# Sums of squares as four rows of 112, and 1 / root spread to all partitions by a store and a load in GpSimd's queue

## The chip, the cores and the metric

The kernel runs on one core of one Trainium2 chip. The metric is the device time of one execution in microseconds. The core's engines are TensorE (PE, with its weight loads shown apart as PEld), VectorE (DVE), ScalarE (ACT) and GpSimd (POOL). Each works through its own list of instructions in the order in which the kernel was written; SyncE (SP) issues most of the transfers. A wait is a semaphore that an instruction needs before it starts.

## What is computed

Three stages in a row, on 4 batches of 448 tokens (1792 tokens) with 768 features:

```python
attn = 1 / (1 + np.exp(-(scale * q @ k.T - np.log(448))))   # 4 batches, 12 heads of 64
x = attn @ v                                                # heads side by side: 1792 x 768
rms = np.sqrt(np.mean(x * x, axis=-1, keepdims=True) + 1e-06)
xn = x / rms * rms_g
g, val = xn @ w_gate, xn @ w_val                            # 768 -> 1536, twice
x = (g * sigmoid(g) * val) @ w_out                          # 1536 -> 768
# then each token goes to the one of 8 experts with the largest logit (768 -> 1024 -> 768)
```

The change is about the line of `rms`: the sum of squares over the 768 features of a token, 1 / root of the mean, and the multiplication of x by it.

## The kernel before

Everything is kept with features on partitions and tokens along the free dimension. x of a batch is six tiles of 128 features x 448 tokens; a feature's sum over partitions can therefore not be made by VectorE, and 1 / root of a token has to stand on all 128 partitions before x can be multiplied by it.

**Attention** runs as one loop of 84 steps, 21 for each batch. A step issues four fp32 matmuls of scores (line 927) into one of two double banks, four fp32 matmuls weights x values (line 944) of the step before last, and one sigmoid on ScalarE (line 933). Both kinds of matmul use 64 x 64 pieces of the array. A group of heads takes four or three steps in turn; its sums are in two banks of a pair, `one0` and `one1` for even groups, `one2` and `one3` for odd ones. When a group ends, ScalarE copies the first bank out (line 971), VectorE adds the second to it (line 972), ScalarE squares the tile (978 or 981) and VectorE adds the square to `ss`, the batch's running sum (line 982). After that a tile of x holds 128 features x 448 tokens, and `ss` 128 partial sums for each token.

**normalise(b)** is a generator that starts at the sixth step of the next batch and goes one `yield` further in every step. For the last batch it goes on in the gated loop, one `yield` at every even slot. It sums `ss` over the partitions with four matmuls that have `ss` as weights and a column of ones as moving data (line 1013), so that the sums of 112 tokens at a time stand on 112 partitions, four columns in all, in bank `one3`. VectorE makes 1 / root of the 112 x 4 numbers in 13 small instructions (lines 1017 to 1030). ScalarE widens each to a row of 128 (`yb`, line 1033), four matmuls against the identity turn this so that each token's number stands on all partitions (line 1038, `one3` again), ScalarE copies it to `rs` (line 1040), and VectorE multiplies the six tiles of x in six steps (line 1043). For batches 2 and 3 SyncE then stores x (line 1048), because it is needed only in the second half of the network.

**Between these** VectorE has other work. A generator `conv` turns the fp64 words of the weights into fp32, three instructions for each piece (lines 217, 221 and 225), one of them in each step that has room: the sets `busy` and `scaling` in the attention loop say which steps have none, and the condition in the gated loop at which slots. SyncE stores each converted piece and loads the next. The calls in `x_at` (x_sum, x_hi, x_lo, lines 320 to 336) make sums and differences of x's tiles and split them into a high and a low part.

**The gated loop** takes batches 0 and 1 through w_gate and w_val: 12 column blocks, each of 7 slots (a Strassen form with seven products), each slot of 9 matmuls of 128 x 128 by 448 (lines 311 to 313). `window(p, n, k)` is what ScalarE and VectorE do beside slot k of block n: they take banks out, form the gate, and prepare the next products' weights (line 282 for the high part, line 287 for the low one, line 304 for sums). Line 450 is the last gate operation of a block, at slot 6; the low part that the second product after it waits for is written a few instructions later. After the gated loop come the projection w_out (`output`), the second half, and the experts.

GpSimd has 11 instructions in the whole run: constants at the start, then nothing until the routing that follows the w_out projection.

## Time and profile before

| | us |
|---|---|
| time, median of 3 runs (890.42 to 890.8) | 890.51 |
| profiled execution, its own time | 890.12 |
| its span | 888.3 |
| PE busy | 877.8 (99%) |
| DVE busy | 645.8 (73%) |
| ACT busy | 396.3 (45%) |
| POOL busy | 4.6 (1%) |

The profiled execution takes 1.8 us more than its span, which lies around the first and last instruction. The granted clock of TensorE is full in all 40 slices of the page. Of the chain that ended last 96% is PE. "Waits" in the views below are times in which an engine had nothing to do until another released it; the chain of waits is followed back from the last instruction, so what stands in it set the end.

### The profile page before, as it was taken

To read this page: it belongs to the slowest core of one execution; us is meant where nothing else is said; L and a number is where in the kernel's file an instruction comes from. 1 tells how busy PE (TensorE), PEld (TensorE's weight loads), DVE (VectorE), ACT (ScalarE), POOL (GpSimd) and SP (SyncE) were. 2 spreads that over 40 slices of the span, in tenths; PEclk is the share of its full clock that TensorE was granted. 3 is DMA by queue.
4 is the path that set the end of the run, shared out by engine and by line. 5 is a ranking of instruction groups with operands and counts; after the bars stand their busy time and mean duration, and the time that the engine had idled before them with its cause. 6 is when DMAs were issued, how large, how long until landed. Compare 5 with 4: busy or idle time off the path is not lost.

```text
span 888.3 us, 14287 instructions
## 1 busy us (share of the span) xinstructions
PE 877.8 (99%) x5376; PEld 737.1 (83%) x5376; DVE 645.8 (73%) x1154; ACT 396.3 (45%) x632; POOL 4.6 (1%) x11
## 2 busy tenths in 40 slices
PE   8999999999999999999999999999999999999997
PEld 3544447999999899999999999998899888889996
DVE  3678889898998985977988788976766644334454
ACT  6877876444445511453444545563322322322220
POOL 0000000000000000000000000000000000000000
PEclk9999999999999999999999999999999999999999
DMA  8988865265544399871212123759779679679232
GB/s 314 397 283 312 300 256 171 81 248 178 178 165 148 135 306 330 271 215 49 72 53 72 54 72 125 257 174 295 204 212 328 221 269 293 195 258 300 76 71 57
DMA packets 121228, 177.59 MB, mean 200 GB/s; under 512 B 62570, under 2 KB 82922, under 8 KB 121153
## 3 DMA queue, kind: packets, MB, share of 16 engines
q1 hardware_dynamic: 111696, 174.03, 59.2%
q10 hardware_dynamic: 9312, 2.07, 1.3%
q8 instruction: 43, 0.70, 0.3%
q0 software_dynamic: 144, 0.53, 0.2%
q14 instruction: 33, 0.26, 0.1%
HBM read 131.11 MB, written 45.35 MB: 199 GB/s over the span
## 4 chain that ended last, share of the span: by engine, by line
PE 96%; DVE 2%; DMA 0%; issue 0%; ACT 0%; SPq 0%; DVEq 0%
PE four L311 14%; PE four L313 14%; PE four L312 14%; PE one L311 12%; PE one L313 12%; PE one L312 12%; PE two L927 7%; PE one L944 7%; PE one L759 1%; DVE m L461 1%; PE four L1291 1%; PE four L1267 1%; PE one L1038 0%; PE one L1013 0%; DMA rqk<-in_qkp 0%; PE one L1291 0%
## 5 line engine op out<-in xcount | busy, mean ns | idle before, releaser
L313 PE MATMUL one<-m,wc 128*128 128x448 f32 x282 | 103.5, 367 | 0.1
L311 PE MATMUL one<-m,wc 128*128 128x448 f32 x282 | 102.6, 364 | 0.0
L312 PE MATMUL one<-m,wc 128*128 128x448 f32 x282 | 102.3, 363 | 0.0
L933 ACT ACTIVATE a<-two,logs 128x896 f32<-128x896 f32 x84 | 84.6, 1008 | 26.7 <-PE two L927 24.1
L927 PE MATMUL two<-rqk 64*64 64x448 f32 x672 | 88.0, 548 | 3.7 <-DMA rqk<-in_qkp 3.7
L944 PE MATMUL one<-a,rv 64*64 64x448 f32 x672 | 86.4, 537 | 0.0
L313 PE MATMUL four<-m,wc 128*128 128x448 f32 x213 | 78.0, 366 | 0.0
L311 PE MATMUL four<-m,wc 128*128 128x448 f32 x213 | 77.7, 365 | 0.0
L312 PE MATMUL four<-m,wc 128*128 128x448 f32 x213 | 77.6, 364 | 0.0
L312 PE MATMUL four<-m,wr 128*128 128x448 f32 x180 | 65.7, 365 | 0.4 <-DVE m L461 0.4
L311 PE MATMUL four<-m,wr 128*128 128x448 f32 x180 | 65.7, 365 | 0.0
L313 PE MATMUL four<-m,wr 128*128 128x448 f32 x180 | 65.5, 364 | 0.0
L287 DVE TENSOR_TENSOR wc<-raw,wc 128x384 fp32r<-128x384 f32 x115 | 61.6, 550 | 3.3 <-ACT wc L282 3.3
L927 PEld LDWEIGHTS two<-rqk 64*64 64x64 f32 x672 | 29.9, 135 | 39.3 <-issue 24.1
L944 PEld LDWEIGHTS one<-a,rv 64*64 64x64 f32 x672 | 30.5, 133 | 33.9 <-issue 32.3
L282 ACT CAST wc<-raw 128x384 fp32r<-128x384 f32 x115 | 55.1, 515 | 7.2 <-DMA raw<-w32d 5.4
L312 PEld LDWEIGHTS one<-m,wc 128*128 128x128 f32 x282 | 52.9, 187 | 4.7
L313 PEld LDWEIGHTS one<-m,wc 128*128 128x128 f32 x282 | 52.9, 188 | 4.1 <-DVE wc L287 0.4
L311 PEld LDWEIGHTS one<-m,wc 128*128 128x128 f32 x282 | 53.0, 188 | 3.8
L1112 ACT CAST w2h<-w2r 128x1024 fp32r<-128x1024 f32 x24 | 25.2, 1048 | 57.3 <-PE one L312 32.3
L311 PE MATMUL four<-xc,wr 128*128 128x448 f32 x126 | 46.8, 372 | 0.0
L312 PE MATMUL four<-xc,wr 128*128 128x448 f32 x126 | 46.2, 367 | 0.0
(279 smaller groups left out, 1923.2 us busy)
## 6 DMA issues: line engine op xcount, KB each, us to landing
raw<-w32d SPq DMA_DIRECT2D x67, 384.0 KB, 3.4
w32d<-wn SPq DMA_DIRECT2D x36, 384.0 KB, 3.1
w1r<-in_w SPq DMA_DIRECT2D x24, 512.0 KB, 5.9
w2r<-in_w SPq DMA_DIRECT2D x32, 384.0 KB, 6.1
x2s<-x SPq DMA_DIRECT2D x48, 224.0 KB, 4.0
rqk<-in_qkp SPq DMA_DIRECT2D x23, 448.0 KB, 6.5
w<-in_wg SPq DMA_DIRECT2D x12, 768.0 KB, 6.8
w<-in_wv SPq DMA_DIRECT2D x12, 768.0 KB, 7.1
```

Source lines behind the costliest of these rows:

```text
L282: nc.scalar.copy(out=h, in_=source(p, n, j).rearrange("p (c k) -> p c k", k=128))
L287: nc.vector.tensor_tensor(out=l, in0=w, in1=f32(h), op=ALU.subtract)
L311: nc.tensor.matmul(p, wh, xh, start=first, stop=False, **kw)
L312: nc.tensor.matmul(p, wh, xl, start=False, stop=False, **kw)
L313: nc.tensor.matmul(p, wl, xh, start=False, stop=last, **kw)
L461: nc.vector.tensor_tensor(out=t, in0=held["h", g, x][0], in1=f32(held["hs", g, x, 0][0]), op=ALU.subtract)
L759: nc.tensor.matmul(logit_bank[b][: 2 * E, :S], gate_2[:, oc, :], x2_t[b, oc][k], start=(oc == (b == B - 1) and k == 1), stop=(oc == KD - 1 ...
L927: nc.tensor.matmul(two[t % 2][o, x, :S], r[head, k : k + D], r[head, :S], start=True, stop=True)
L933: nc.scalar.activation(out=a, in_=two[t % 2][:, :, :S], func=AF.Sigmoid, bias=logs, scale=1.0 / math.sqrt(D))
L944: nc.tensor.matmul(one[2 * y + k][halves[x], :S], v4[halves[i], c, x, :], a[halves[i]], start=(c == first), stop=(c == end))
L1112: nc.scalar.copy(out=hv, in_=r)
L1267: nc.tensor.matmul(ph[TS * j : TS * j + TS], xt[:, c, :], ph2["w1f"][:, c, n * j : n * j + n], start=(c == 0), stop=(c == KD - 1),)
```

## The change

The four matmuls that sum `ss` change sides. The weights are now four columns of a new constant `part` (the c-th of four has ones in column c and zeros elsewhere), and `ss` is the moving data: 4 x 112 results accumulate in one place of `one3`, row c for tokens 112 c to 112 c + 111. The same 13 instructions of VectorE work on 4 x 112 numbers in place of 112 x 4. GpSimd's queue then stores them as 448 numbers in DRAM (`rsd`) and loads them with a broadcast into `rs`, all 128 partitions. The widening, the four turning matmuls and the two ScalarE copies are gone. x is multiplied from the seventh `yield` after that on, four steps later than before. `scaling` moves by four steps with it, one call of `x_sum` by one, and `busy` follows.

```diff
+    add("part", np.tile(np.eye(NC).reshape(1, -1), (128, 1)))
...
+    rsd = [dram.tile([1, S], F32, name=f"rsd{b}") for b in range(B)]
...
-        pm = mi[:CT, :NC]
+        pm = mi[:NC, :CT]
         for c in range(NC):
-            nc.tensor.matmul(pm[:, c : c + 1], ss[:, c * CT : (c + 1) * CT], ones[:, 0:1], start=True, stop=True)
-        va = rp.tile([CT, NC], F32, tag="va", name="va")
-        ya = rp.tile([CT, NC], F32, tag="ya", name="ya")
-        ta = rp.tile([CT, NC], F32, tag="ta", name="ta")
+            nc.tensor.matmul(
+                pm, const("part")[:, c * NC : (c + 1) * NC], ss[:, c * CT : (c + 1) * CT], start=(c == 0), stop=(c == NC - 1)
+            )
+        t = keep.tile([NC, 3, CT], F32, tag="xr", name="ya")
+        va, ya, ta = (t[:, i, :] for i in range(3))
...
         yield
-        yb = keep.tile([CT, NC, 128], F32, tag="xr", name="yb")
-        nc.scalar.copy(out=yb, in_=ya.unsqueeze(2).to_broadcast([CT, NC, 128]))
-        yield
-        yield
-        pr = mi[:, :S]
-        for c in range(NC):
-            nc.tensor.matmul(pr[:, c * CT : (c + 1) * CT], yb[:, c, :], ident[:CT, :CT], start=True, stop=True)
+        nc.gpsimd.dma_start(out=rsd[b].rearrange("o (c p) -> (o c) p", p=CT), in_=ya)
         rs = rp.tile([128, S], F32, tag="rs", name="rs")
-        nc.scalar.copy(out=rs, in_=pr)
-        yield
+        nc.gpsimd.dma_start(out=rs, in_=rsd[b].to_broadcast([128, S]))
+        for _ in range(7):
+            yield
         for c in range(KD):
...
-        60: [(x_sum, 0, P5)], 62: [(x_sum, 0, P7)], 64: [(x_hi, 0, P5, True)], 65: [(x_lo, 0, P5)],
+        61: [(x_sum, 0, P5)], 62: [(x_sum, 0, P7)], 64: [(x_hi, 0, P5, True)], 65: [(x_lo, 0, P5)],
...
-    busy = {8, 14, 18, 23, 28, 40, 43, *range(60, 73, 2), 67, 71, 81}
+    busy = {8, 14, 18, 23, 28, 40, 43, 61, *range(62, 73, 2), 67, 71, 81}
...
-        scaling = n >= QS and n % QS in (10, 12, 14)
+        scaling = n >= QS and n % QS in (14, 16, 18)
```

Step 81 stands both in `busy` and in the new `scaling`, so one more step of the attention loop has a conversion, and every later conversion comes one place earlier. Line numbers of the changed kernel are 2 higher up to the middle of `normalise` and 2 lower after it.

On TensorE, in the step of batch 1 where the turning matmuls of batch 0 stood, this is the order before (`two` and `one` are banks, `a` the weights of attention, `rv` the values):

```order
L927 MATMUL two_147<-rqk 64x448 x4
L944 MATMUL one_143<-a,rv 64x448
L944 MATMUL one_144<-a,rv 64x448 x2
L944 MATMUL one_143<-a,rv 64x448
L1038 MATMUL one_146<-cst,yb 128x112 x4
L927 MATMUL two_148<-rqk 64x448 x4
```

and now:

```order
L929 MATMUL two_151<-rqk 64x448 x4
L946 MATMUL one_147<-a,rv 64x448
L946 MATMUL one_148<-a,rv 64x448 x2
L946 MATMUL one_147<-a,rv 64x448
L929 MATMUL two_152<-rqk 64x448 x4
```

The four matmuls between the two halves of the loop are gone; the four of the sums stay at their place, with other shapes.

On VectorE, from the last of the 1 / root instructions of batch 0 to the first multiplication of x, before (`wn` is a converted weight, `m` a tile of x):

```order
L1030 SCALAR_TENSOR_TENSOR ya<-ta,ya 112x4
L217 TENSOR_SCALAR wn<-w_454 128x768
L221 SCALAR_TENSOR_TENSOR wn<-w_454,wn 128x768
L972 TENSOR_TENSOR m<-one_145,m 128x448
L225 SCALAR_TENSOR_TENSOR wn<-w_454,wn 128x768
L1043 SCALAR_TENSOR_TENSOR m<-m,ng_sb,rs 128x448
```

and now:

```order
L1033 SCALAR_TENSOR_TENSOR ya<-ta,ya 4x112
L219 TENSOR_SCALAR wn<-w_458 128x768
L223 SCALAR_TENSOR_TENSOR wn<-w_458,wn 128x768
L974 TENSOR_TENSOR m<-one_149,m 128x448
L227 SCALAR_TENSOR_TENSOR wn<-w_458,wn 128x768
L219 TENSOR_SCALAR wn<-w_502 128x768
L984 TENSOR_TENSOR ss<-ss,sq 128x448
L223 SCALAR_TENSOR_TENSOR wn<-w_502,wn 128x768
L227 SCALAR_TENSOR_TENSOR wn<-w_502,wn 128x768
L974 TENSOR_TENSOR m<-one_148,m 128x448
L219 TENSOR_SCALAR wn<-w_581 128x768
L1041 SCALAR_TENSOR_TENSOR m<-m,ng_sb,rs 128x448
```

Ten instructions stand where four stood; the first multiplication now comes behind the next group's addition (line 972, now 974) and a third conversion.

On VectorE in the gated loop, from line 450 of block 2 (now 452) on, before, with two multiplications of x of batch 3 in the block:

```order
L450 SCALAR_TENSOR_TENSOR m<-m,one_143 128x448
L287 TENSOR_TENSOR wc<-sw,wc 128x384
L1043 SCALAR_TENSOR_TENSOR m<-m,ng_sb,rs 128x448
L221 SCALAR_TENSOR_TENSOR wn<-w_1401,wn 128x768
L388 TENSOR_TENSOR c_1801<-four_1490,c_1801 128x448
L287 TENSOR_TENSOR wc<-raw,wc 128x384
L1043 SCALAR_TENSOR_TENSOR m<-m,ng_sb,rs 128x448
L225 SCALAR_TENSOR_TENSOR wn<-w_1401,wn 128x768
L400 TENSOR_TENSOR m<-c_1801,m 128x448
L401 SCALAR_TENSOR_TENSOR m<-m,c_1836 128x448
```

and now, with the first two of the four that stand in the same block:

```order
L452 SCALAR_TENSOR_TENSOR m<-m,one_147 128x448
L289 TENSOR_TENSOR wc<-sw,wc 128x384
L1041 SCALAR_TENSOR_TENSOR m<-m,ng_sb,rs 128x448
L227 SCALAR_TENSOR_TENSOR wn<-w_1352,wn 128x768
L390 TENSOR_TENSOR c_1779<-four_1475,c_1779 128x448
L289 TENSOR_TENSOR wc<-raw,wc 128x384
L1041 SCALAR_TENSOR_TENSOR m<-m,ng_sb,rs 128x448
L219 TENSOR_SCALAR wn<-w_1416 128x768
L402 TENSOR_TENSOR m<-c_1779,m 128x448
L403 SCALAR_TENSOR_TENSOR m<-m,c_1809 128x448
```

Before, four of batch 3's six multiplications stood between line 450 of blocks 1 and 2 and two between blocks 2 and 3; now none stands before line 452 of block 2, four stand between blocks 2 and 3, and two between blocks 3 and 4.

## Rows read from the trace of the kernel before

**Rows 1.** Waits of TensorE, whole span: us in total, times, longest us.

```profile
PE two L927 <- DMA rqk<-in_qkp: 3.7, 1, 3.7
PE four L312 <- DVE m L461: 0.4, 1, 0.4
```

**Rows 2.** Chain that ended last, batch 0's normalise: start us, us, what.

```profile
45.55 0.88 PE one L1013 x8
46.43 0.91 PE two L927 x8
47.34 0.75 PE one L944 x8
...
52.60 1.07 PE one L1038 x8
54.59 0.75 PE one L944 x8
```

**Rows 3.** TensorE's timeline, batch 3's normalise, gated loop: start us, us, instruction.

```profile
150.90 0.85 PE L1013 MATMUL one<-ones,ss 128*112 128x1 f32 x8
...
151.91 0.36 PE L312 MATMUL one<-m,wc 128*128 128x448 f32 x1
152.11 0.36 PE L313 MATMUL one<-m,wc 128*128 128x448 f32 x1
...
164.44 1.04 PE L1038 MATMUL one<-cst,yb 112*128 112x112 f32 x8
...
165.54 0.36 PE L312 MATMUL one<-m,wc 128*128 128x448 f32 x1
```

**Rows 4.** Weight loads by line: ns least/median/most, first and last start, shape.

```profile
L759 PEld LDWEIGHTS one<-x,gate x48: 93/94/96, 315.4 to 629.6; 128*16 128x16 f32 x48
...
L1013 PEld LDWEIGHTS one<-ones,ss x32: 173/178/179, 45.5 to 151.5; 128*112 128x112 f32 x32
```

**Rows 5.** VectorE by line: ns least/median/most, first and last start, shape.

```profile
L1017 DVE TENSOR_SCALAR va<-one x4: 152/162/163, 46.5 to 151.9; 112x4 f32<-112x4 f32 x4
...
L1043 DVE SCALAR_TENSOR_TENSOR m<-m,ng_sb,rs x24: 674/678/686, 54.3 to 183.6; 128x448 f32<-128x448 f32 x24
```

**Rows 6.** VectorE's timeline, attention, batch 1: start us, us, instruction, [idle before].

```profile
49.98 0.17 DVE L1030 SCALAR_TENSOR_TENSOR ya<-ta,ya 112x4 f32<-112x4 f32 x1
...
59.19 0.62 DVE L972 TENSOR_TENSOR m<-one,m 128x448 f32<-128x448 f32 x1 [0.68 <-ACT m L971]
...
62.24 0.62 DVE L982 TENSOR_TENSOR ss<-ss,sq 128x448 f32<-128x448 f32 x1 [0.37 <-ACT sq L981]
...
64.24 0.62 DVE L972 TENSOR_TENSOR m<-one,m 128x448 f32<-128x448 f32 x1
```

**Rows 7.** TensorE's timeline in the same place: the bank's next use.

```profile
67.94 0.93 PE L944 MATMUL one<-a,rv 64*64 64x448 f32 x8
```

**Rows 8.** GpSimd's DMA issues: tiles, queue, count, us to landing.

```profile
xg<-x2d,s_g POOLq DMA_INDIRECT x1, 7.5
out<-rows,s_s1st POOLq DMA_INDIRECT x1, 3.0
```

**Rows 9.** Windows: us, busy us (instructions) by engine, clock, DMA share, GB/s.

```profile
83.00:93.00 10.00, 10.00 (x108) 4.43 (x104) 7.59 (x16) 8.47 (x12) 0.00 (x0) 1.00 0.97 341
...
684.00:694.00 10.00, 10.00 (x51) 9.19 (x50) 8.84 (x24) 1.26 (x2) 1.12 (x1) 1.00 0.99 342
```

**Rows 10.** VectorE's timeline, gated loop, blocks 2 and 3.

```profile
180.09 0.62 DVE L450 SCALAR_TENSOR_TENSOR m<-m,one 128x448 f32<-128x448 f32 x1
...
186.22 1.02 DVE L287 TENSOR_TENSOR wc<-raw,wc 128x384 fp32r<-128x384 f32 x2
...
192.96 0.62 DVE L450 SCALAR_TENSOR_TENSOR m<-m,one 128x448 f32<-128x448 f32 x1
```

**Rows 11.** TensorE's timeline there: the matmul that reads that low part.

```profile
187.58 0.37 PE L313 MATMUL four<-m,wc 128*128 128x448 f32 x1
```

**Rows 12.** GpSimd's timeline, the first transfer of rows 8: start us, us, instruction.

```profile
686.18 1.12 POOL L1235 DMA_INDIRECT xg<-x2d,s_g  x1 [56.06 <-DMA w2r<-in_w]
```

## The prediction, blind

> **What bounds the kernel now.** I read the waits of TensorE first, over the whole span. There are three, and the two long ones are 3.7 us at the start for the first load and 0.4 us for VectorE at the end of the first gated loop [rows 1]; 96% of the chain that ended last is TensorE. The kernel is one unbroken stream of matmuls: whatever leaves the stream shortens the run by its own length, provided that the other engines, which have little room in places, still deliver in time. The chain then shows what normalise costs the stream [rows 2], the timeline of TensorE the same for the last batch, which falls into the gated loop [rows 3], and the timelines of VectorE how much room there is.
>
> **What the stream loses.** In attention a half step is 0.75 us. From the start of the four sums (45.55) to the next L944 (47.34) it takes 1.79 us where 0.75 would do, so the sums cost 1.04 us; the turning matmuls cost 54.59 - 52.60 - 0.75 = 1.24 us [rows 2]. Both figures include what the L927 behind them is longer than 0.75. The chain shows the same for the two other batches whose normalise is in attention. In the gated loop the pace is 0.20 us a matmul. There the sums start at 150.90 and the second matmul behind them at 151.91, which is 1.01 - 0.20 = 0.81 us for the sums; in the same way 165.54 - 164.44 - 0.20 = 0.90 us for the turning [rows 3]. Removing the turning matmuls gives 3 x 1.24 + 0.90 = 4.6 us.
>
> **What the new sums cost.** They remain eight instructions on TensorE, with 4 weight columns and 112 moving ones in place of 112 and 1. No row shows four columns. A load of 16 columns took 94 ns and one of 112 took 178 [rows 4], so the loads get short; the moving side becomes that of the turning matmuls, which cost 0.90 with a longer load than either. So the new sums lie between half of the old (loads alone, 0.4) and the turning (0.9), in attention between 0.5 and 1.24. I take the old cost, which is nearer to the upper row because the moving side is the same: no gain or loss here, at most 3 x 0.2 + 0.1 = 0.7 us worse or 3 x 0.5 + 0.4 = 1.9 us better.
>
> **ScalarE** loses two copies a batch. It never held TensorE up, so this is worth nothing by itself.
>
> **VectorE, the 13 small instructions.** Four numbers a partition took 0.16 us, 448 took 0.68 [rows 5]; on a straight line 112 take 0.29, so 13 instructions cost 13 x 0.13 = 1.7 us more for each batch, at most (none, if the length of the dependence hides it). VectorE waited for the sums before its L1017 in attention, so the first of them is still on time there, and 1.7 us fit into the idle time of each batch's steps. In the gated loop the room before L450 of block 1 takes them.
>
> **The store and the load.** They stand alone in GpSimd's queue, the load behind the store's landing; nothing else is queued behind them until the routing. What waits is VectorE's first L1041, and behind it on VectorE the addition that empties a bank of attention. Batch 0 as example. The last root instruction ended at 50.15 [rows 6]; with the longer instructions 51.8. The first multiplication now stands behind the addition that came at 59.19; TensorE is 1.24 earlier by then, so that addition ends at 58.5 and, behind one conversion of about half a microsecond, the multiplication is due at 59.0. That gives 7.2 us free. Behind it comes L982, which waited for ScalarE until 62.24 and now comes at 61.0: a multiplication of 0.6 us may start as late as 60.4 without delaying anything. Then the addition at 64.24, whose bank TensorE writes next at 67.94 [rows 7], has (with both 1.24 earlier) about 3.2 us before TensorE waits. So the way through DRAM may take 60.4 + 3.2 - 51.8 = **11.8 us**. The other two batches give 11 to 12 in the same manner, and the last one, in the gated loop, over 20.
>
> The only transfers that GpSimd issues before took 3.0 and 7.5 us to land [rows 8]. The long one ran while the DMA engines were 99% busy; where batch 1's pair would fall they are at 97% [rows 9]. The store is 1.8 KB, the load 224 KB and plain, with longer rows than the gathered one. I take 3.0 + 5.5 = 8.5 us, between 3.0 + 3.0 = 6.0 and 7.5 + 7.5 = 15.0. At 8.5 VectorE waits about a microsecond where it would have waited anyway, and TensorE doesn't.
>
> The page "DMA: Bandwidth & Descriptors" of the Trainium skill, section "Anatomy of one DMA — SWDGE (gpsimd) path", gives 2.0 us plus the bytes over 436 KB per us; by that the pair is an estimated 4.5 us and never late. The trace doesn't agree: 386 KB would take 2.9 us by it and took 7.5 [rows 8]. The sum would be the same by the page.
>
> **The multiplications, four steps later.** In attention each lands in steps with as many conversions moved out. At the end, batch 2's six share steps 77 to 82 with the first gated weights, but two conversions have been moved ahead; what TensorE needs first from VectorE there has about 2.5 us of room. In the gated loop it is tight. Between L450 of blocks 2 and 3 VectorE was busy without a break: 12.87 us [rows 10]. TensorE needs 12.73 for the 63 matmuls of a block (165.54 - 151.91 - 0.90 for the turning [rows 3]). Two multiplications stood there, now four: 2 x 0.68 = 1.36 us more [rows 5], so L450 of block 3 comes about 1.5 us late. The low part behind it was written 0.81 us before it was read: L287 at 186.22 took 0.55 of its 1.02, read at 187.58 [rows 10, 11]. Two long conversions stood ahead of it there; in block 4 one of the two is a short one, so that there is somewhat more. TensorE waits 1.5 - 0.81 = 0.7 us at most; I take **0.3 us**, with 0 as the other end.
>
> **The conversion that moved ahead** puts a short instruction (L217) where a long one (L221) stood at the end of that loop, in front of VectorE's only long-lasting backlog; the wait of 0.4 us [rows 1] goes, or stays.
>
> **Sum:** 4.6 + 0.4 - 0.3 = 4.7 us less. The profiled execution would go from 890.12 to 885.4, the median of 890.51 to **885.8**. The bounds of the parts give 4.6 - 0.7 - 0.7 = 3.2 to 4.6 + 1.9 + 0.4 = 6.9 less: 883.6 to 887.3, of which I believe the lower end least, since nothing but load time speaks for it.
>
> **Rivals.**
> *VectorE becomes the bound around the gated loop's first five blocks.* For it: VectorE has no idle time in blocks 2 and 3 [rows 10], the 1.7 us of longer root instructions fall just ahead, and the late L450 delays ScalarE too. If the backlog lasts through blocks 3 and 4 at 1 to 1.5 us each, TensorE waits 2 to 3 us: 888. Against it: blocks 1 and 2 become emptier by four multiplications.
> *GpSimd and VectorE stop each other.* If VectorE stood still for each GpSimd instruction (1.12 us [rows 12]), two a batch, it would lose 2.2 us a batch. Attention covers that; the last batch's would fall on blocks 0 and 1, where about 1.8 us of room is left for the root instructions' 1.7: 1.5 to 2.2 us, 887.6. That such a lock exists is what the page "SBUF — State Buffer" says, section "Who interferes with whom": GpSimd and a VectorE instruction in a two-port mode share a port pair, and the later one waits until the other is through. No row here shows the two at once.
> *The way through DRAM is late.* The point is 11.8 us; at 15.0 the addition behind the multiplication is 3.2 us late in three batches, 9.6 us in all, and the run takes 885.8 + 9.6 = **895.4**, slower than before. It decides from 11.8 + 4.7 / 3 = 13.4 us on. For it: three of the four pairs run beside weight loads that keep the DMA engines nearly full, and a GpSimd transfer did take 7.5 us under such a load [rows 8, 9]. Against it: the store is tiny, and the two rows added give 10.5.
> *The stream doesn't get shorter,* because new sums cost as much as old sums and turning together, for instance when four columns make the array run badly: 890.
>
> **How the numbers follow.** A measurement of this kernel can tell about 0.2% (1.8 us) from no change. Forecast 0.66; VectorE the bound 0.13; GpSimd against VectorE 0.06; late way 0.12, of which half reaches the slower side and the rest ends between; no shorter stream 0.03. The forecast's cases and most of the next two lie below 888.7: faster 0.83. Within 0.2%: what remains of these, part of the late way, and the last: 0.10. Slower: 0.07. The range leaves out the late way, the last rival and the low end of the sums: 884.4 to 888.6.
>
> **What would show it.** In the changed profile, TensorE's chain at batches 0 to 2 should show one piece of eight with 0.8 to 1.0 us in each batch and none of L1038; attention should end 3.5 to 4 us earlier. L1041's first wait for the load should be under 1.5 us, and no PE wait should name L974 or a bank. In the gated loop a PE wait of under 0.7 us for L289 may stand near block 4, and the wait at the end of that loop should be gone. The prediction is wrong if GpSimd's pair takes over 12 us, if the new sums cost over 1.2 us, or if PE waits for VectorE sum up to over 1.5 us.

## The result: 899.3 us, and the profile after

The changed kernel takes 899.28 us (median of 6 runs, 896.15 to 899.99), the kernel before in the same comparison 890.46 (890.07 to 890.80): a ratio of 1.0088 [1.0077, 1.0098], slower by 8.8 us where 4.7 us of gain were forecast. The time lies outside the range, on the side of the rival "the way through DRAM is late" (895.4). The profiled execution took 899.5 us, its span grew from 888.3 to 897.7.

In the waits of TensorE over the whole span (us in total, times, longest) five kinds are new, the wait for rqk (attention's loads) has grown by 0.5, and the 0.4 us at the end of the first gated loop [rows 1] is gone:

```profile
PE two L929 <- DMA rqk<-in_qkp: 4.2, 2, 3.9
PE two L929 <- ACT a L935: 2.1, 4, 0.7
PE one L313 <- ACT four L372: 2.0, 1, 2.0
PE one L313 <- ACT c L399: 1.6, 1, 1.6
PE one L946 <- DVE m L974: 0.9, 1, 0.9
PE one L1015 <- DVE ss L984: 0.4, 2, 0.3
```

(Lines have moved a little: L929, L935, L946, L974, L983 and L984 are L927, L933, L944, L972, L981 and L982 of before; L372 and L399, L370 and L397 of before, are ScalarE's copies of banks in the gated stage; L1015 are the sums, L1033 the last kind of root instruction, L1035 the store, L1037 the load, L1041 the multiplications.)

What was forecast for TensorE's own work came true. In the chain the sums of batch 0 are one piece of eight (start us, us, what), as long as the old ones, 0.88 [rows 2], and nothing stands where the turning was:

```profile
45.60 0.87 PE one L1015 x8
```

Ten of the 13 root instructions on 112 elements cost VectorE 0.26 us each in place of 0.16 [rows 5], the other three 0.20 (two kinds of the ten: line, ns least/median/most, first and last start):

```profile
L1020 DVE TENSOR_SCALAR ya<-one x4: 255/258/262, 46.5 to 159.8; 4x112 f32<-4x112 f32 x4
L1031 DVE TENSOR_TENSOR ya<-ya x12: 253/263/265, 48.7 to 164.4; 4x112 f32<-4x112 f32 x12
```

The way through DRAM did not. GpSimd's timeline (start us, us, instruction, idle before and for what) has a pair for each batch, and the windows under it, each from a store's issue to its load's, show how full the DMA engines were meanwhile (after the granted clock: DMA share, GB/s):

```profile
51.64 0.69 POOL L1035 DMA_DIRECT2D rsd<-ya  x1 [51.18 <-DVE ya L1033]
57.30 0.59 POOL L1037 DMA_DIRECT2D rs<-rsd  x1 [4.97 <-DMA rsd<-ya]
86.58 0.53 POOL L1035 DMA_DIRECT2D rsd<-ya  x1 [28.69 <-DVE ya L1033]
94.24 0.56 POOL L1037 DMA_DIRECT2D rs<-rsd  x1 [7.12 <-DMA rsd<-ya]
...
165.52 0.53 POOL L1035 DMA_DIRECT2D rsd<-ya  x1 [36.92 <-DVE ya L1033]
167.66 0.56 POOL L1037 DMA_DIRECT2D rs<-rsd  x1 [1.61 <-DMA rsd<-ya]
```

```profile
51.64:57.30 5.66, 5.66 (x64) 2.29 (x60) 5.23 (x8) 4.56 (x6) 0.69 (x1) 1.00 0.92 335
86.58:94.24 7.66, 7.66 (x88) 3.12 (x84) 6.16 (x10) 6.24 (x8) 0.53 (x2) 1.00 1.00 368
122.20:128.04 5.84, 5.84 (x68) 2.32 (x64) 5.80 (x7) 4.74 (x7) 1.05 (x1) 1.00 0.97 379
165.52:167.66 2.14, 0.81 (x4) 0.77 (x5) 1.93 (x5) 1.82 (x4) 0.53 (x2) 1.00 0.01 1
```

The store of 1.8 KB alone kept the load waiting 5.0, 7.1 and 4.8 us in attention, where the engines were 92 to 100% busy, and 1.6 us in the gated loop, where they stood idle. VectorE doesn't part the two cases: it was busy for 80 to 99% of these windows in attention and for 90% of the quiet one. The load took 3.5 to 6.8 us. From the end of the root to the first multiplication it was 12.8, 14.6 and 10.8 us in the three batches of attention; 8.5 had been taken and 11.8 allowed. VectorE's timeline shows the first multiplication of batches 0, 1 and 2 waiting:

```profile
64.13 0.68 DVE L1041 SCALAR_TENSOR_TENSOR m<-m,ng_sb,rs 128x448 f32<-128x448 f32 x1 [5.06 <-DMA rs<-rsd]
...
100.92 0.68 DVE L1041 SCALAR_TENSOR_TENSOR m<-m,ng_sb,rs 128x448 f32<-128x448 f32 x1 [5.40 <-DMA rs<-rsd]
...
132.66 0.69 DVE L1041 SCALAR_TENSOR_TENSOR m<-m,ng_sb,rs 128x448 f32<-128x448 f32 x1 [1.77 <-DMA rs<-rsd]
```

How this comes to TensorE shows in ScalarE's timeline. ScalarE's square of a head stands in its list ahead of the next sigmoids and needs VectorE's addition L974, which stood behind the waiting multiplication; so the sigmoids are late:

```profile
67.38 0.58 ACT L983 ACTIVATE sq<-m 128x448 f32<-128x448 f32 x1 [1.67 <-DVE m L974]
67.87 1.89 ACT L935 ACTIVATE a<-two,logs 128x896 f32<-128x896 f32 x2
```

TensorE, in its own timeline, waits for the first of these sigmoids:

```profile
68.91 0.98 PE L929 MATMUL two<-rqk 64*64 64x448 f32 x8 [0.54 <-ACT a L935]
```

SyncE carries it on in a second way. Its list holds the store of converted weights (L232), which waits for VectorE's conversions, and behind it the next loads for attention (rqk). After 59.9 us it stood until 69.43; in the kernel before the same store went out at 64.36 us (before, then now):

```profile
64.36 0.33 SPq L230 DMA_DIRECT2D w32d<-wn  x1
```

```profile
59.03 0.86 SPq L210 DMA_DIRECT2D w<-in_wv  x1
69.43 0.33 SPq L232 DMA_DIRECT2D w32d<-wn  x1
69.87 0.37 SPq L898 DMA_DIRECT2D rv<-in_v  x1
70.69 0.32 SPq L891 DMA_DIRECT2D rqk<-in_qkp  x1
```

### The profile page after: what moved, and what is told of

The parts are those of the page before. It is cut to its first block, busy times and chain, and to the rows that moved or that the text cites. A ratio compares the mean times of both kernels' runs of the same rounds, so it can differ in the third digit from the quotient of the medians.

```text
span 897.7 us, 14232 instructions
## 1 busy us (share of the span) xinstructions
PE 879.8 (98%) x5344; PEld 727.9 (81%) x5344; DVE 649.2 (72%) x1154; ACT 391.9 (44%) x624; POOL 9.6 (1%) x19
## 4 chain that ended last, share of the span: by engine, by line
PE 85%; DVE 8%; DMA 5%; issue 1%; ACT 0%; SPq 0%; POOLq 0%; DVEq 0%
PE four L313 14%; PE four L314 14%; PE four L315 14%; PE one L313 12%; PE one L314 12%; PE one L315 12%; PE two L929 3%; PE one L946 2%; DMA rs<-rsd 2%; DMA rsd<-ya 2%; PE one L761 1%; DVE m L1041 1%; DVE m L326 1%; DVE wn L227 1%; DVE m L974 1%
## 5 line engine op out<-in xcount | busy, mean ns | idle before, releaser
L935 ACT ACTIVATE a<-two,logs 128x896 f32<-128x896 f32 x84 | 84.2, 1007 | 26.7 <-PE two L929 25.2
L929 PE MATMUL two<-rqk 64*64 64x448 f32 x672 | 84.3, 554 | 6.3 <-DMA rqk<-in_qkp 4.2
L946 PE MATMUL one<-a,rv 64*64 64x448 f32 x672 | 82.2, 538 | 0.9 <-DVE m L974 0.9
L289 DVE TENSOR_TENSOR wc<-raw,wc 128x384 fp32r<-128x384 f32 x115 | 61.7, 550 | 5.1 <-ACT wc L284 5.1
L929 PEld LDWEIGHTS two<-rqk 64*64 64x64 f32 x672 | 26.4, 135 | 46.7 <-issue 26.7
L946 PEld LDWEIGHTS one<-a,rv 64*64 64x64 f32 x672 | 26.8, 134 | 39.1 <-issue 35.0
```

Source lines behind the costliest of these rows:

```text
L289: nc.vector.tensor_tensor(out=l, in0=w, in1=f32(h), op=ALU.subtract)
L929: nc.tensor.matmul(two[t % 2][o, x, :S], r[head, k : k + D], r[head, :S], start=True, stop=True)
L935: nc.scalar.activation(out=a, in_=two[t % 2][:, :, :S], func=AF.Sigmoid, bias=logs, scale=1.0 / math.sqrt(D))
L946: nc.tensor.matmul(one[2 * y + k][halves[x], :S], v4[halves[i], c, x, :], a[halves[i]], start=(c == first), stop=(c == end))
```

## The experiments

All are compared by one ladder: how far the same instruction of TensorE lies behind (+) or ahead of (-) its time in the profile of the kernel before, at three places. "Gated" is the first matmul of the gated stage (138.74 us before), "four" the first into the second set of banks from converted weights (147.26; behind the stage's first stall), "output" the first of the output stage (294.97). Where two or three profiles of a kernel exist, each stands. Three kernels that leave TensorE's attention as it was (before_pair, moved, before_pad) lie 0.2 to 0.4 us behind at "gated", so the ladder can't tell less than that. The rows of "gated", before and in the changed kernel's first profile:

```profile
138.74 0.47 PE L311 MATMUL one<-m 128*128 128x448 f32 x1
```

```profile
141.92 0.47 PE L313 MATMUL one<-m 128*128 128x448 f32 x1
```

| run | gated | four | output | median us | ratio to before |
|---|---|---|---|---|---|
| changed kernel | +3.2 / +0.9 / +1.1 | +5.4 / +4.6 / +4.7 | +9.6 / +5.8 / +7.8 | 899.28 | 1.0088 [1.0077, 1.0098] |
| no_dram, no_dram_2 | -3.7 / -3.3 | -1.8 / +0.2 | +0.8 / +0.7 | - | - |
| no_wait, no_wait_2 | -0.8 / -1.9 | +1.1 / +0.1 | +3.1 / +4.6 | - | - |
| before_pair | +0.4 | +0.4 | +0.4 | 890.46 | 0.9998 [0.9988, 1.0007] |
| moved | +0.4 | +3.9 | +3.9 | 894.03 | 1.0038 [1.0024, 1.0052] |
| later | +0.8 | +0.8 | +1.6 | 892.64 | 1.0025 [1.0014, 1.0036] |
| later_pool | -0.3 | -0.3 | +5.0 | 894.98 | 1.0036 [1.0019, 1.0054] |
| after_b2 | -0.6 | -0.5 | +6.7 | 897.82 | 1.0077 [1.0054, 1.0100] |
| after_b2_pool | +1.4 | +1.6 | +8.8 | 898.56 | 1.0070 [1.0049, 1.0090] |
| rows_spread | -0.1 | 0.0 | +1.0 | 893.39 | 1.0029 [1.0015, 1.0044] |
| fast_spread | +4.4 | +4.4 | +7.2 | 904.17 | 1.0146 [1.0122, 1.0171] |
| before_pad | +0.2 | +0.2 | +0.5 | 890.64 | 1.0000 [0.9989, 1.0011] |

### The wait for the roots, and the transfers without it

```diff
 no_dram
-        nc.gpsimd.dma_start(out=rsd[b].rearrange("o (c p) -> (o c) p", p=CT), in_=ya)
-        nc.gpsimd.dma_start(out=rs, in_=rsd[b].to_broadcast([128, S]))
+        nc.gpsimd.memset(rs, 0.5)
 no_wait
-                out=xt[c], in0=xt[c], scalar=ng_sb[:, c : c + 1], in1=rs, op0=ALU.mult, op1=ALU.mult
+                out=xt[c], in0=xt[c], scalar=ng_sb[:, c : c + 1], in1=ones[:, 0:1].to_broadcast([128, S]), op0=ALU.mult, op1=ALU.mult
```

> The changed kernel without the way through DRAM: GpSimd sets rs to a constant instead of the store and the load, so the roots reach nothing and x is scaled by g and a constant. All else, the new sums, the root on 112 elements and the scaling four steps later, is kept. Theory 1 (the multiplication waits for a way through DRAM that takes 11 to 15 us instead of the 8.5 of the prediction, and VectorE's wait comes back to TensorE by way of ScalarE's squares): no wait at L1041, the time falls to about 886 (885 to 888). Theory 2 (the new shape or the later steps cost the time themselves: 13 root instructions of 0.3 us in place of 0.2, scaling in among the sums for the next stage): it stays at 894 or more. Theory 3 (the GpSimd transfers get in the way of others, nobody's wait): also about 886, so the next run has to part it from theory 1.

> The changed kernel with its store and load as they are, but the multiplication takes a column of ones in place of rs: the transfers run, nobody waits for the load, and the roots reach nothing. Theory 1: within 1 us of the run without the transfers, about 886. Theory 3 (the transfers hold VectorE's port or take the DMA engines from the weights): it stays near the changed kernel, 894 to 899.

> The run without the transfers once more (the roots are replaced by a constant). No wait in the attention, which ends 3.5 to 3.9 us ahead of the kernel before, and a wait of 1.9 us at the start of the gated stage. The total again says nothing.

> The run without a wait once more (transfers as in the changed kernel, the multiplication takes ones in place of the roots). If the transfers themselves cost the attention: TensorE waits for rqk in it again and the attention ends 0 to 1.5 us ahead of the kernel before. If the first profile was chance: 3 to 4 us ahead, as without the transfers. The total says nothing, since without the roots the tokens go to other experts.

Their totals (979.7 and 982.2 us) can't be used: without the roots the routing comes out differently, and the 90 us that are added lie after 700 us (before that, no_dram is 1.0 us and no_wait 4.0 us behind). Up to there they can be read by the ladder. Without the transfers attention has not one wait of TensorE and ends 3.7 and 3.3 us ahead: the gain that was forecast for it is there. With the transfers running and nobody waiting it ends 0.8 and 1.9 us ahead, and TensorE waits for rqk, as the second profile's waits show beside those at the start of the gated stage:

```profile
PE two L929 <- DMA rqk<-in_qkp: 4.6, 2, 3.7
PE one L313 <- ACT four L372: 1.9, 1, 1.9
PE one L313 <- ACT c L399: 1.6, 1, 1.6
...
```

So the transfers by themselves cost some 2.1 us of attention (the means of two profiles each; 1.4 to 3.0), and the wait for them 3.1 us more (mean of the changed kernel's three, +1.7, against -1.4). The expected "within 1 us of the run without the transfers" failed: theory 1 alone was not enough. It failed for no_dram too, which lies 0.8 us behind at "output" where about 4.5 ahead was expected. What both runs share is a wait of 1.9 us at the start of the gated stage and one of up to 1.6 behind it, with no wait for roots anywhere, so those belong to something else.

A wait cost more than its idle time. In the changed kernel's first profile TensorE's waits in attention, without the first load's, add up to 3.9 us, but at "gated" it lies 6.9 us behind no_dram. Matmul by matmul against no_dram it falls back by 1.15 us at the wait of 0.54 us (68.9 us) and by 0.95 us at the one of 0.72 us (139.5 us). Why is not shown.

> The kernel before with the two GpSimd transfers added and nobody waiting for them: right after ScalarE's copy of the root 4 rows of 112 of that copy go to DRAM and from there to all partitions of a tile that is dead by then. Computes what the kernel before does. If the transfers crowd the loads of the attention (theory: in the run without a wait TensorE stood at rqk and attention ended 2.9 us later than without the transfers), TensorE waits for rqk once or twice, attention ends 1.5 to 3 us later and the time is 892 to 893.5. If they cost nothing by themselves and only the wait for them does: 890.5.

```diff
         nc.scalar.copy(out=yb, in_=ya.unsqueeze(2).to_broadcast([CT, NC, 128]))
+        nc.gpsimd.dma_start(out=rsd[b].rearrange("o (c p) -> (o c) p", p=CT), in_=yb[:NC, 0, :CT])
+        rx = keep.tile([128, S], F32, tag=("k0", "k1", "k3", "xs")[b], name="rx")
+        nc.gpsimd.dma_start(out=rx, in_=rsd[b].to_broadcast([128, S]))
```

In the kernel before the same two transfers cost nothing: 890.46 us, and in attention no wait but the first load's. The two results fit together if the loads of attention have about as much to spare as its steps are long: in the kernel before they come in time beside the transfers, and in a stream that is 1.24 us a batch faster they don't. That is how I read it; what the rows show is the wait for rqk in the one case and none in the other. It also speaks against the rival "GpSimd and VectorE stop each other": eight such transfers changed no time.

### The four steps

```diff
 moved: the kernel before, old sums and turning
         nc.scalar.copy(out=rs, in_=pr)
         yield
+        for _ in range(4):
+            yield
...
-        scaling = n >= QS and n % QS in (10, 12, 14)
+        scaling = n >= QS and n % QS in (14, 16, 18)
```

> The kernel before with nothing changed but the steps: its scaling four steps later, as in the changed kernel, with the old sums, root and turning matmuls. Theory 1: the roots are there 4 steps ahead, the multiplication waits for nothing, 890 to 891.5, no change. Theory 2 (the later steps are the cost): 894 or more.

This run has none of the new sums, transfers or waits for roots (the steps without a conversion and one x_sum move with the multiplications), and it loses 3.5 us (1.0038 [1.0024, 1.0052]): neither theory's number, and a cause of its own. Up to the gated stage the ladder says +0.4, no more than before_pair has; behind the stage's first stall +3.9, and it stays there. ScalarE's timeline of the kernel before (one line), the same of this run (two), and TensorE's timeline of this run (one):

```profile
140.64 0.58 ACT L981 ACTIVATE sq<-m 128x448 f32<-128x448 f32 x1 [1.99 <-DVE m L972]
```

```profile
142.96 0.58 ACT L981 ACTIVATE sq<-m 128x448 f32<-128x448 f32 x1 [3.78 <-DVE m L972]
143.44 0.53 ACT L370 COPY four<-one 128x448 f32<-128x448 f32 x1
```

```profile
144.02 0.74 PE L311 MATMUL one<-m 128*128 128x448 f32 x1 [1.87 <-ACT four L370]
```

The last heads' additions L972 now stand behind two multiplications of batch 2 and a conversion in VectorE's list; ScalarE's square waits 3.78 us for one, and the copy L370 that frees a bank for TensorE stands behind the square. The other 1.6 us are the clock. In the windows (granted clock third from the right) TensorE stood from 142.15 to 144.02 and went on at 0.50, the lower of its two levels (1.2 GHz), for 3 us:

```profile
142.00:144.00 2.00, 0.15 (x4) 0.00 (x0) 2.00 (x4) 1.04 (x3) 0.00 (x0) 1.00 0.93 339
144.00:147.00 3.00, 2.98 (x8) 2.68 (x9) 2.39 (x5) 2.46 (x4) 0.00 (x0) 0.50 0.83 250
```

The same wait of 1.9 or 2.0 us stands in the changed kernel, no_dram and no_wait. The clock fell behind it in this run, in no_dram_2 and in two of the changed kernel's three profiles, not in the others; what decides is not shown.

### More room for the way, and batch 2 alone

```diff
 later: the changed kernel
-        for _ in range(7):
+        for _ in range((11, 11, 10, 7)[b]):
             yield
 after_b2: the changed kernel
+        for _ in range((7, 7, 10, 7)[b]):
 later_pool, after_b2_pool: also
-                nc.sync.dma_start(
+                (nc.gpsimd if b == 2 else nc.sync).dma_start(
```

(In all four the steps without a conversion move as well; in later and later_pool also the copies and differences that read x for the gated stage.)

> The changed kernel with the multiplications 4 steps later still in batches 0 and 1 and 3 later in batch 2 (a step is about 1.6 us), the work that reads x for the gated stage moved behind them by as much. Computes what the changed kernel does. Theory 1: VectorE's wait at L1041 goes from 5.1, 5.4 and 1.8 us to under 1 us in batches 0 and 1 and to nothing in batch 2; attention ends 5 us or more earlier than in the changed kernel; the time is 888 (886 to 891), since more of VectorE's work comes into the start of the gated stage. Theory 2: the later steps cost more, 899 or above.

With three or four more steps of room no multiplication waits, and TensorE's waits shrink to these:

```profile
PE two L929 <- DMA rqk<-in_qkp: 5.7, 2, 3.9
PE one L313 <- ACT c L399: 0.9, 1, 0.9
PE one L1015 <- DVE ss L984: 0.5, 1, 0.5
PE four L314 <- DVE m L463: 0.3, 1, 0.3
```

The time falls by 6.6 us, to 892.6. So the late way and the place of the multiplications were worth that much together; but it is 1.6 us above the range expected, and still slower than the kernel before. A wait of 1.9 us for rqk takes the place: the conversions had moved too, SyncE stood at the store of one until 123.76 us and issued the load behind it, at 126.54.

> The changed kernel with one move taken back in part: batch 2's multiplications start 3 steps later still, so that most of them come behind the last head's addition in VectorE's order; batches 0, 1 and 3 are as in the changed kernel. Theory: the wait of TensorE for ScalarE's copy at the start of the gated stage (2.0 us in the changed kernel, 1.9 in the three other kernels with that move) is gone and the first matmul of the gated stage into the four banks comes as far behind the kernel before as the end of attention does, not 2.1 us farther; attention itself ends 2.5 to 3.5 us late as before, since the first two batches still wait; 896 to 898 in all. If that wait hangs on the late end of attention and not on the order, it stays, and the time is 899.

The wait for the copy is gone, as the theory said (the ladder's "gated" and "four" agree). Attention ended 0.6 us ahead in this profile where 2.5 to 3.5 late was expected; single profiles of the changed kernel lie 2.3 us apart there. The time came out as expected, but for another reason. In its waits of TensorE a new one stands in the place of the one removed, and the second of the gated stage stays:

```profile
...
PE one L313 <- ACT wc L284: 2.3, 1, 2.3
PE one L313 <- ACT c L399: 1.6, 1, 1.6
...
```

The first is for the gated stage's first weights from DRAM. In the chain they hang on a load of words to convert (w<-in_wv) that SyncE issued at 143.73 us, just ahead of theirs (144.30) and right behind a store of x that waits for batch 2's last multiplication. So I asked whether that store holds the loads up.

> The run with batch 2's multiplications three steps later, with batch 2's two stores of x in GpSimd's queue in place of SyncE's and nothing else changed. If SyncE, standing at the store of x, held up the gated stage's first weights: the last weight load is issued at about 142 us instead of 143.7, the first weights are there 1.5 us or more earlier and TensorE's wait for ScalarE's copy of them falls from 2.3 us to under 1; the time falls by 1 to 2 us, to 895 to 897. If the loads are late for another reason (VectorE's conversion of the last weights, which the store ahead of the load waits for): the wait stays at 2 us or more and the time at 897 to 898.

> The run with more room in all three batches, with the same two stores in GpSimd's queue. SyncE stood there from 132.4 to 143.1 us at the two stores and issued the gated stage's weights behind them. If they held the weights up: ScalarE's copy of the first of them comes before 146.5 us instead of 147.7, the wait of 0.9 us in the gated stage falls to under 0.5, and the time is 891 to 892. If not: 892.6 as it was.

It doesn't, in after_b2: with the stores in GpSimd's queue the load goes out at 143.94 us, since the store of converted weights just ahead of it (143.56) waits for VectorE all the same; the time is unchanged (898.6). That guess of mine fell. TensorE's wait for ScalarE's copy did fall from 2.3 to 0.7 us, but with attention ending 2.0 us later in this profile and the copy no earlier (150.97 us against 150.45), and a wait of 1.5 us for another copy (L419) stands behind it. In later it did: the first weights were copied at 145.47 instead of 147.72 us, but the waits behind them (1.6 and 1.0 us) and the spacing of the matmuls (below) took back more, 895.0 us. What holds is that VectorE's first work on the weights from DRAM (L287, at 145.92 us before; now L289) is further behind its time in the kernel before than TensorE's "four" is, by 2.6 us in the changed kernel, 3.0 in no_dram and 1.6 in later (0.8 in moved), and that one operand or another is then late. VectorE waits there for ScalarE's copy of these weights (2.9 us in the changed kernel), so the lateness comes with the weights. Which edit would bring them in time stays open.

### The new sums without DRAM

```diff
 rows_spread: the kernel before with the new sums and root, and
-            nc.tensor.matmul(pr[:, c * CT : (c + 1) * CT], yb[:, c, :], ident[:CT, :CT], start=True, stop=True)
+            nc.tensor.matmul(
+                pr[:, c * CT : (c + 1) * CT], ident[:NC, c : c + 1].to_broadcast([NC, 128]), ya, start=True, stop=True
+            )
```

> The new sums and the root on 4 rows of 112 with no DRAM and no moved step: the rows are spread to all partitions by 4 matmuls with one-hot weights of 4 rows, at the step where the kernel before turns its copy; ScalarE's 512-wide copy goes. Computes what the kernel before does. If the new shape is harmless (theory 1): TensorE's attention as before, no wait at the start of the gated stage, in batch 3 a wait of at most 1 us behind the longer root: 890 to 891.5. If the shape of the sums or the root is itself dear: 893 or more.

The new sums and the root cost attention nothing (ladder 0.0 up to "four"), and the longer root brings no wait in batch 3. There VectorE reached L389, the instruction behind the nine of the root, at 157.55 us and ScalarE's copy behind it came at 158.68, just in time; in the changed kernel the same pair (L390, L399) came at 165.16 and 166.28 us, and TensorE waited 1.6 us. So the longer root alone doesn't make the 1.6 us; it takes a VectorE that is already late. Whether that lateness would do it without the longer root no run shows. The median, 893.4 us with a range of 891.1 to 895.7, is above what was expected; the one profile (891.1, the fastest run) accounts for 1.0 us by the output stage, and the rest I can't show.

> As the run before it in batches 0 to 2, but the rows are laid on a diagonal (one VectorE product, a rounded copy by ScalarE, the rest by VectorE) and spread by two reduced-precision matmuls of 448, high part and rest; batch 3 is left as in the kernel before. No DRAM, no moved step. A turn of 1.24 us on TensorE becomes some 0.6 (two matmuls of 448 at the 0.20 us of the gated stage's, and the handover), three times: attention 1.5 to 2.5 us shorter, 888 to 889, if VectorE's two more instructions of 448 in a batch (about 0.6 us each) keep out of the way. If VectorE is the limit there: 890.5 or more.

```diff
 fast_spread, batches 0 to 2
+        nc.vector.tensor_tensor(
+            out=yd, in0=ya.unsqueeze(1).to_broadcast([NC, NC, CT]),
+            in1=ident[:NC, :NC].unsqueeze(2).to_broadcast([NC, NC, CT]), op=ALU.mult,
+        )
+        nc.scalar.copy(out=hi, in_=yd)
...
+        nc.vector.tensor_tensor(out=lo, in0=yd, in1=f32(hi), op=ALU.subtract)
...
+        for i, y in enumerate((hi, lo)):
+            nc.tensor.matmul(
+                pr, one_r.to_broadcast([NC, 128]), y.rearrange("k c p -> k (c p)"), start=(i == 0), stop=(i == 1)
+            )
```

904.2 us, the slowest of all. The two matmuls are short (0.46 and 0.36 us in TensorE's timeline), but ScalarE's rounded copy stands in its list ahead of a sigmoid and of the copy that frees the bank (L974), and waits for VectorE's product; TensorE waited for the bank 4.1 us in all. Behind the first of these waits (1.66 us) its granted clock was 0.50 from 55.8 to 59.2 us, which cost 1.7 us more. Attention ends 4.4 us late by both. Most of the rest is the longer step of the matmuls (below), which this profile keeps from 150 to about 600 us, where it is 12.7 us behind. It is the link of the changed kernel again, in ScalarE's timeline and then in TensorE's:

```profile
52.14 0.56 ACT L1043 CAST yh<-ya 4x448 fp32r<-4x448 f32 x1 [1.89 <-DVE ya L1039]
```

```profile
54.06 0.46 PE L1049 MATMUL one<-yh,one_r 4*128 4x448 f32 x1 [1.66 <-ACT m L974]
```

No version of mine beats the kernel before.

### The spacing of the matmuls

```diff
 before_pad
+    add("part", np.tile(np.eye(NC).reshape(1, -1), (128, 1)))
 after_a, after_b: the changed kernel unaltered
```

> The kernel before with the 16 columns of the new constant and nothing that uses them, which moves the tiles behind the constants by 64 bytes. In the gated stage a matmul of 448 follows the last in 202.7 ns in all kernels with that constant and in 202.2 without it. If the place of the tiles does it: 202.7 here and 1 to 1.5 us more, 891.5 to 892. If the other changes do it: 202.2 and 890.5.

> The changed kernel unaltered, looked at once more, for the spacing of matmuls in the gated stage, 206.7 ns in its first profile from 165 to 311 us and 202.7 in most of the others. If that spacing makes the two groups of its times (896.2 and 896.7; 899.2 to 900.0): a run near 896.4 has 202.7 there and one near 899.5 has 206.7. If not, the spacing is the same in both.

> As the run before it, once more, to have both groups: 896.4 with 202.7 ns or 899.5 with 206.7 ns.

In the gated stage a matmul of 448 starts 202.2 ns after the last in the kernel before, before_pair and moved, and 202.7 in before_pad and most other kernels with the 16 columns of constants: their place does that. By the routing, at 411 us, before_pad is 1.0 us behind, 0.2 of it from the start; the time shows nothing of it (ratio 1.0000 [0.9989, 1.0011]), so the 1 us expected in the total was not there. In its profile it grows to 1.6 us by 650 us and falls back to 0.4 at the end.

The larger step is within one kernel. After_a took 896.5 us, after_b 897.7, and TensorE's timeline shows the first and the tenth of a run of matmuls at the same place of each (after_a, then after_b):

```profile
200.16 0.36 PE L313 MATMUL one<-m,wc 128*128 128x448 f32 x1
...
201.98 0.36 PE L313 MATMUL four<-m,wc 128*128 128x448 f32 x1
```

```profile
200.48 0.37 PE L313 MATMUL one<-m,wc 128*128 128x448 f32 x1
...
202.34 0.37 PE L313 MATMUL four<-m,wc 128*128 128x448 f32 x1
```

Nine steps take 1.82 us in one and 1.86 in the other, 202.7 and 206.7 ns, at a granted clock of 1.00 in both. After_b went over to the long step at 165 us, right at its wait for L399, and kept it until the output stage, 144 us later: about 700 matmuls at 4.0 ns, 2.8 us. The ladder from "four" to "output" has +1.2 us in after_a and +3.1 in after_b. The changed kernel's first profile (899.5 us), after_b2, after_b2_pool and later_pool have it from that wait on as well, no_dram, no_dram_2, no_wait, later and after_a don't, and no_wait_2 takes it up at 203 us with no wait near. Of the kernels without a wait there, before, before_pair, before_pad, moved and rows_spread keep the short step from 160 us on; fast_spread has the long one from 150 to about 600. What sets it was not settled, nor that the two groups of times are nothing else: after_b lies between them.

## Why the prediction was wrong, step by step

- **What the stream loses** held: without the transfers attention ends 3.7 and 3.3 us ahead, against 3 x 1.24. **What the new sums cost** held too (0.87 us against 0.88 [rows 2]), and so did that **ScalarE's** lost copies are worth nothing and that the **0.4 us** at the loop's end goes (0.2 of it stands in after_a).
- **The 13 small instructions** took about the length forecast in attention (the root of batch 0 ended at 51.3, 51.8 was said), but the sentence that the room before L450 takes them in the gated loop was wrong for a VectorE that comes late: TensorE waited 1.6 us.
- **The store and the load: the step that failed first.** I took 3.0 + 5.5 = 8.5 us, the 3.0 from a transfer with the DMA engines busy for less than half of the time (share 0.38 from 826 to 834 us), because the store is tiny; the way took 12.8, 14.6 and 10.8 us. Its size didn't decide: 5.0, 7.1 and 4.8 us beside engines at 92 to 100% busy, 1.6 us beside idle ones. I had the rows that said so, 7.5 us for a transfer beside engines at 99% and 97% of them busy where batch 1's pair would fall [rows 8, 9], and used it as an end of the range only. By 7.5 for the store and 5.5 for the load the way would have been 13 us. The Trainium skill, "DMA: Bandwidth & Descriptors", section "Anatomy of one DMA — SWDGE (gpsimd) path", prices such a transfer at 2.0 us and its bytes; that is near the 1.6 us of the quiet case, and the trace disagrees for the busy one.
- **What a late way costs** was followed along one path only, from the addition to the bank that TensorE writes next. Two shorter ones were missed: ScalarE's square, which stands ahead of the next sigmoid in an ordered list and waits for the same addition, and SyncE's store of converted weights, which stands ahead of the next loads. So the allowance of 11 to 12 us was too long: batch 2's way of 10.8 us was inside it, and TensorE waited 0.7 us for a sigmoid behind it; behind batch 0's 12.8 us its first wait was for a sigmoid, not for the bank. The rival "the way through DRAM is late" had the right cause and sign; with the measured ways its own formula gives 1.0 + 2.8 + 0 = 3.8 us in place of its 9.6; in the means of the profiles attention lost 3.1 by the wait and some 2.1 with the transfers alone, where TensorE waits for rqk, which was no term at all.
- **The multiplications, four steps later** was given 2.5 us of room at the end of attention. There was none: moved, with the old sums and turning, lost 3.5 us (1.9 of waiting, 1.6 by the clock), and I had not followed ScalarE's L981, which already waited 1.99 us for VectorE there in the kernel before. The forecast wait at block 4 (0.3) was looked for at the wrong place. The rival "VectorE becomes the bound around the gated loop's first five blocks" came near in size, 2.0 + 1.6 us of waits there against its 2 to 3, but the first of them came from the end of attention and not from the load of blocks 2 and 3.
- **No term at all** was what came behind some stalls: the lower clock for 3 us (1.6 us), and the longer step of the matmuls (some 3 us), whose cause is open.

For the first profile of the changed kernel the account is: attention +3.2 in place of -3.7; the gated stage's first wait 2.2 to "four"; from there to the output stage +4.3, of which the second wait is 1.6, the longer step about 3.1 (4.5 ns in 202.2 over some 140 us), the turning that is gone -0.9, and 0.5 unaccounted for. That makes +9.6, and +9.4 at the end.

## What to carry to other kernels

Price a small transfer by how busy the DMA engines are when it runs, not by its bytes: here a store of 1.8 KB kept its load waiting 1.6 us beside idle engines and 4 to 7 beside full ones. Before you move work on an engine that runs in order, list who waits for what stands behind it, on every engine and in SyncE's list of transfers; the shortest of these paths sets the room, not the one that leads to TensorE's next bank. In a stream without gaps each stall may cost more than its length: 1.15 us for one of 0.54 here, and 3.5 for one of 1.9 where the clock fell too.

## What the runs showed of the hardware that was not expected

- A store of 1.8 KB from GpSimd's queue kept the load behind it waiting 4.2 to 7.1 us in attention beside DMA engines 84 to 100% busy, and 1.4 to 1.6 us when the DMA share was 0.01 (in later also in attention, at 118 us).
- Matmuls of 448 columns at a full granted clock come 202.2, 202.7 or 206.7 ns apart, and keep one of these for 100 us and more. The first step follows the place of the tiles; the last comes and goes, often at a wait, and is not explained.
- After a wait of 1.9 or 2.0 us TensorE's granted clock was 0.50 (1.2 GHz) for about 3 us in four profiles, and in fast_spread after one of 1.66; it stayed at 1.00 in other profiles after waits of 1.8 to 2.3 us.
